# Zero-padded keys written by GpSimd, one crossbar DMA per head pair, and the gain product on ScalarE

## The chip, the cores and the metric

The kernel runs on one core of one Trainium2 chip. The metric is the device time of one execution in microseconds (us); lower is better. The median of three runs before the change is 489.74 us (489.65 to 492.26).

## What is computed

The reference is an attention with normalised queries and keys, followed by a two-layer network with a sigmoid gate. In short:

```python
def rmsnorm(x, g):
    rms = np.sqrt(np.mean(x * x, axis=-1, keepdims=True) + 1e-06)
    return x / rms * g
q_n, k_n = rmsnorm(q, g_q), rmsnorm(k, g_k)          # (8, 12, 448, 64)
scores = 1.0 / np.sqrt(64) * q_n @ k_n.transpose(0, 1, 3, 2)
attn = softmax(scores)
x = (attn @ v).transpose(0, 2, 1, 3).reshape(3584, 768)
h = x @ w_in                                          # 768 x 2048
out = (h * (1.0 / (1.0 + np.exp(-1.702 * h)))) @ w_out
```

Both gains act on the 64 channels of a head that the score product sums over. So g_q and g_k may be multiplied together and applied once, to the queries or to the keys.

## The kernel before, in words

**Tiling.** The attention works on 48 pairs of heads: 8 batches with 6 pairs each, and `i` numbers the pairs. A pair's 448 rows are 4 blocks of 112. Its two heads have 64 channels each, which fill 128 partitions once they are turned. The network follows batch by batch: for each of 8 batches 16 tiles of `w_in` (L485), and for two batches together 7 row tiles of `w_out` (L508).

**One pair, step by step.** `load` (L237, L242) brings q, k and v, from SyncE's queue (SP). `square` (L247) on ScalarE and `reduce` (L253) on VectorE give sums of squares. `seed` on VectorE and `rsqrt` on GpSimd make the inverse root, for three pairs together. `norm` (L291), on GpSimd, multiplies q (`gi` 0) and k (`gi` 1) and writes bf16 rows `qkn`, ordered by block, head and channel. Then the rows are turned, so that the channels lie on the partitions:

- pairs 0 to 11 (`ON_PE`): `turn_pe` (L309) on TensorE, `take_q` (L314) and `take_k` (L319) on VectorE;
- pairs 12 to 47: `turn_dma` (L326), a crossbar DMA in SyncE's queue that turns 8 blocks of 128 columns (4 of queries, 4 of keys) into `qT`, and then `pad` (L333) on VectorE, twice. Each `pad` copies the 64 partitions of one head's keys out of `qT` into `kz`, with the gains multiplied in. The other 64 partitions of each half of `kz` are zero from the start (L186, L187).

`score` (L343) multiplies `kz` with `qT` over all 128 partitions. The zero half keeps the other head out of the sum. `expo` (L348) on ScalarE takes the exponential, `values` (L355) multiplies with v, `divide` (L365, L366) on VectorE normalises, and a second crossbar DMA (L385) turns the result into `xT`, the input of the network. In the network, `tanh` (L494) runs on ScalarE, `gate` (L500) on VectorE, `take_out` (L518) on ScalarE.

**Rings.** `kz` and `qT` have 3 buffers each, `qkn` has 3, `raw` (the loaded q and k) has 7. A transposition of pair i therefore waits for the last score product of pair i-3, `norm` of pair i for the transposition of pair i-3, and the load of pair i for `norm` of pair i-7.

**What sets the order.** The order on each engine is written out ahead of the run by a planner, `_Order`. Each task has an engine, a planned duration, a key, and names that it depends on. The planner plays time forward, and a free engine takes the ready task with the smallest key. Each engine then runs its list in that order, so a late task holds back all that stands behind it in the same list. The planned durations matter for the order alone:

```python
for hp in range(2):
    od.add(("K", i, hp), "DVE", 540, lambda i=i, hp=hp: pad(i, hp), i - 2.5,
           deps=[("T", i)] + kz_free)
```

Here a `pad` is planned with 540 ns. The key of a score product is `i + kc / 4`, that of network work grows by 1 for every 5800 ns of planned matmuls. So TensorE's list interleaves network matmuls with attention. The network's work left over after the last pair makes up the end of the program.

Of the kernel before, what the change touches and what calls it, by code (L numbers as in the profile page):

```python
# [10 lines left out]
BF16 = mybir.dt.bfloat16  # L11
I32 = mybir.dt.int32
ALU = mybir.AluOpType
# [113 lines left out]
def kernel(  # L127
# [43 lines left out]
    for t, src in ((gq, g_q), (gk, g_k)):  # L171
        col = src.rearrange("(d o) -> d o", o=1)
        for lo in (0, 64):
# [1 line left out]
    gG = consts.tile([128, 1], FP32)  # L175


    N_ATT, N_KZ, N_V, N_RAW, N_SQ, N_QKN, N_QT = 3, 3, 4, 7, 2, 3, 3
    att_ring = [consts.tile([128, NS, 2, AW], BF16, name=f"att{j}", tag=f"att{j}")
                for j in range(N_ATT)]  # L180
    kz_ring = [consts.tile([128, 2, NS * SS], BF16, name=f"kz{j}", tag=f"kz{j}")
               for j in range(N_KZ)]
    vx_ring = [consts.tile([128, 2, NS, D + 1], BF16, name=f"vx{j}", tag=f"vx{j}")
               for j in range(N_V)]
    for t in kz_ring:
        nc.vector.memset(t[64:128, 0, :], 0.0)  # L186
        nc.vector.memset(t[0:64, 1, :], 0.0)  # L187
    for t in vx_ring:
        nc.gpsimd.memset(t[:, :, :, D:D + 1], 1.0)
    for t in att_ring:  # L190
# [8 lines left out]
    sq_p = pool("sq", N_SQ)  # L199
    stat_p = pool("stat", 3)  # L200
    small_p = pool("small", 2)
    qkn_p = pool("qkn", N_QKN)
    qT_p = pool("qT", N_QT)
    obs_p = pool("obs", 2)
    xt_p = pool("xt", 3)
    g_p = pool("g", 1)
# [16 lines left out]
            return link[0] - now + 500.0  # L223
        return lat

    raw, vraw, rs, qkn, qT, obs, xT = {}, {}, {}, {}, {}, {}, {}
    groups = [[0], [1], [2], [3, 4, 5]] + [list(range(j, j + 3)) for j in range(6, NG, 3)]
    group_of = {p: g for g in groups for p in g}
    ssq_of, sq_of = {}, {}
# [56 lines left out]

    def norm(i, gi):
        y, a = rs[i]
        if gi == 0:
            qkn[i] = qkn_p.tile([128, 2, NS, 2, D], BF16, tag="qkn", name="qkn")  # L290
        nc.gpsimd.tensor_tensor(  # L291
            out=qkn[i][:SS, gi],
            in0=raw[i][:SS, gi].rearrange("p h n d -> p n h d"),
            in1=y[:SS, a, gi].rearrange("p h n -> p n h").to_broadcast([SS, NS, 2, D]),
            op=ALU.mult)

    def vcast(i):
        vx = vx_ring[i % N_V][:SS].rearrange("p h n d -> p (h n) d")
# [6 lines left out]
    def turn_pe(i):  # L305
        tps[i] = ps_w.tile([128, 2, NS, SS], BF16, tag="w", name="t_ps")
        for gi in range(2):
            for s in range(NS):
                nc.tensor.transpose(tps[i][:, gi, s, :], qkn[i][:SS, gi, s, :, :],  # L309
                                    ident[:SS, :SS])  # L310

    def take_q(i):
        qT[i] = qT_p.tile([128, 2, NS * SS], BF16, tag="qT", name="qT")
        nc.vector.tensor_copy(out=qT[i][:, 0, :],  # L314
                              in_=tps[i][:, 0].rearrange("p n s -> p (n s)"))

    def take_k(i, hp):
        r = slice(64 * hp, 64 * hp + 64)
        nc.vector.tensor_scalar(out=kz_ring[i % N_KZ][r, hp, :],  # L319
                                in0=tps[i][:, 1].rearrange("p n s -> p (n s)")[r],  # L320
                                scalar1=gG[r, :], scalar2=None, op0=ALU.mult)

    def turn_dma(i):

        qT[i] = qT_p.tile([128, 2, NS * SS], BF16, tag="qT", name="qT")
        nc.sync.dma_start_transpose(  # L326
            out=qT[i][:, :, :].rearrange("p g (n s) -> p (g n) s", s=SS),
            in_=qkn[i][:SS].rearrange("s g n h d -> s (g n h d)"))

    def pad(i, hp):  # L330

        r = slice(64 * hp, 64 * hp + 64)
        nc.vector.tensor_scalar(  # L333
            out=kz_ring[i % N_KZ][r, hp, :].rearrange("p (n s) -> p s n", s=SS),
            in0=qT[i][r, 1, :].rearrange("p (n s) -> p s n", s=SS),
            scalar1=gG[r, :], scalar2=None, op0=ALU.mult)

    scs, os_ = {}, {}

    def score(i, kc):  # L340
        sc = scs[i, kc] = ps_sc.tile([128, 2, 512], FP32, tag="sc", name="sc")
        for hp in range(2):
            nc.tensor.matmul(sc[:SS, hp, :S],  # L343
                             lhsT=kz_ring[i % N_KZ][:, hp, kc * SS:(kc + 1) * SS],
                             rhs=qT[i][:, 0, :], start=True, stop=True)

    def expo(i, kc):
        nc.scalar.activation(out=att_ring[i % N_ATT][:SS, kc, :, :S],  # L348
# [47 lines left out]
    for i in range(NG):  # L396
        b = i // NP
        for w in range(3):
            od.add(("L", i, w), "ACTQ" if i == 0 and w == 1 else "SP", 400,
                   lambda i=i, w=w: load(i, w), i - 7 + 0.1 * w,  # L400
                   deps=[("V", i - N_RAW)] if w == 2 else [("N", i - N_RAW, 0), ("N", i - N_RAW, 1)],
                   lat=moved(830.0))
        parts = [slice(0, 1), slice(1, 2)] if i < 2 else [slice(0, 2)]
        for j, part in enumerate(parts):
            od.add(("S", i, j), "ACT", 920 / len(parts) + 80,
                   lambda i=i, p=part: square(i, p), i - 3,
                   deps=[("L", i, w) for w in range(part.start, part.stop)]
                   + [("R", i - N_SQ, 0), ("R", i - N_SQ, 1)])
            od.add(("R", i, j), "DVE", 1210 / len(parts) + 50,
                   lambda i=i, p=part: reduce(i, p), i - 2.8, deps=[("S", i, j)])  # L410
        if i == group_of[i][-1]:
            od.add(("Q0", i), "DVE", 400, lambda g=group_of[i]: seed(g), i - 2.7,
                   deps=[("R", p, j) for p in group_of[i] for j in range(2)])
            od.add(("Q", i), "POOL", 2300 if len(group_of[i]) > 1 else 1700,
                   lambda g=group_of[i]: rsqrt(g), i - 2.6, deps=[("Q0", i)])
        for gi in range(2):
            od.add(("N", i, gi), "POOL", 1080, lambda i=i, gi=gi: norm(i, gi), i - 2.4,
                   deps=[("Q", group_of[i][-1]), ("T", i - N_QKN)])
        od.add(("V", i), "POOL", 1000, lambda i=i: vcast(i), i - 1.6,
               deps=[("L", i, 2), ("P", i - N_V, 1, NS - 1)])  # L420
        kz_free = [("C", i - N_KZ, NS - 1)]
        if i < ON_PE:
            od.add(("T", i), "PE", 400, lambda i=i: turn_pe(i), i - 1.0,
                   deps=[("N", i, 0), ("N", i, 1)], lat=250, takes=("w", ("K", i, 1)))
            od.add(("KQ", i), "DVE", 400, lambda i=i: take_q(i), i - 2.0,
                   deps=[("T", i), ("C", i - N_QT, NS - 1)])
            for hp in range(2):
                od.add(("K", i, hp), "DVE", 460, lambda i=i, hp=hp: take_k(i, hp), i - 1.9,
                       deps=[("T", i), ("KQ", i), ("gG"), ("K", i, hp - 1)] + kz_free)
        else:  # L430
            od.add(("T", i), "SP", 400, lambda i=i: turn_dma(i), i - 10.0,
                   deps=[("N", i, 0), ("N", i, 1), ("C", i - N_QT, NS - 1)], lat=moved(1600.0))
            for hp in range(2):
                od.add(("K", i, hp), "DVE", 540, lambda i=i, hp=hp: pad(i, hp), i - 2.5,
                       deps=[("T", i)] + kz_free)
        for kc in range(NS):
            od.add(("C", i, kc), "PE", 380, lambda i=i, kc=kc: score(i, kc), i + kc / 4,
                   deps=[("K", i, 0), ("K", i, 1), ("KQ", i)], lat=250,
                   takes=("sc", ("E", i, kc)))
            od.add(("E", i, kc), "ACT", 917, lambda i=i, kc=kc: expo(i, kc), i + kc / 4 - 1,  # L440
                   deps=[("C", i, kc), ("P", i - N_ATT, 1, NS - 1)])
        for hp in range(2):
            for qs in range(NS):
                od.add(("P", i, hp, qs), "PE", 130, lambda i=i, hp=hp, qs=qs: values(i, hp, qs),
                       i + 0.8 + hp / 2 + qs / 8,
                       deps=[("E", i, kc) for kc in range(NS)] + [("V", i)]
                       + [("P", i, hp, qs - 1)], lat=250,
                       takes=("o", ("O", i, hp)) if qs == 0 else None)
            od.add(("O", i, hp), "DVE", 630, lambda i=i, hp=hp: divide(i, hp), i - 2,
                   deps=[("P", i, hp, NS - 1), ("B", i - 2)])  # L450
        xt_free = [("M", b - 3)] if i % NP == 0 else [("X", i - 1)]
        if i < ON_PE:
            od.add(("B", i), "PE", 200, lambda i=i: back_pe(i), i + 1.5,
                   deps=[("O", i, 0), ("O", i, 1)], lat=250, takes=("w", ("X", i)))
            od.add(("X", i), "DVE", 390, lambda i=i: take_x(i), i - 1, deps=[("B", i)] + xt_free)
        else:
            od.add(("X", i), "SP", 400, lambda i=i: back_dma(i), i - 10,
                   deps=[("O", i, 0), ("O", i, 1)] + xt_free, lat=moved(800.0))
            od.add(("B", i), "none", 0, lambda: None, i, deps=[("X", i)])
# [144 lines left out]
```

## Time and profile before

| | |
|---|---|
| median of 3 runs | 489.74 us |
| the profiled execution: its own time | 490.08 us |
| the profiled execution: span from first to last instruction | 488.3 us |
| mean granted TensorE clock | 0.982 of full speed |
| DMA | 63.36 MB in 95342 packets, mean 130 GB/s |

The rows of the profile come from the profiled execution. Engines: PE is TensorE's matmuls, PEld its weight loads, DVE is VectorE, ACT is ScalarE, POOL is GpSimd, SP is SyncE, whose queue (SPq) issues most DMAs. "o L355 <- DVE obs L366" means that the instruction of line 355, which writes `o`, started late because it had to wait for line 366 on DVE. A number in brackets at the end of a timeline row is the idle time of that engine just before the row, and what ended it.

### The profile page before, as it was taken

The numbers are of one execution on the slowest core, as the hardware profiler recorded it, in microseconds if no ns is written. First come the engines' busy times: TensorE is split into PE (matmuls) and PEld (weight loads), VectorE is DVE, ScalarE is ACT, GpSimd is POOL, SyncE is SP. The second block draws the span as 40 slices with busy tenths as digits, with TensorE's granted clock in tenths as the row PEclk, the third lists the DMA queues.
The fourth block names the chain that finished last, engine by engine and source line by source line (L and its number), as shares of the span: only waits on it lengthen the run. The fifth ranks groups of instructions, "written<-read, shape, count | busy, mean of one in ns | idle before, by whom it ended". The sixth has DMA issues, their size and how long they took to land.

```text
span 488.3 us, 9605 instructions
## 1 busy us (share of the span) xinstructions
PE 440.4 (90%) x3728; PEld 271.5 (56%) x3728; DVE 324.2 (66%) x536; ACT 305.1 (62%) x427; POOL 236.5 (48%) x327
## 2 busy tenths in 40 slices
PE   0667999987998898999989999989999999999995
PEld 0345666654565464566555565556666666565563
DVE  4478888995885568977888659966696636512500
ACT  3585998756785377775866667856676557723421
POOL 2899787596365364646546566656344310000000
PEclk9986999999999799999999999999999999999999
DMA  8999999646554458366464576454412432012022
GB/s 201 235 244 250 253 243 212 174 100 161 123 133 122 135 130 170 86 152 168 126 161 89 150 182 143 125 119 124 107 30 51 101 71 62 20 43 66 0 66 65
DMA packets 95342, 63.36 MB, mean 130 GB/s; under 512 B 54336, under 2 KB 91712, under 8 KB 95296
## 3 DMA queue, kind: packets, MB, share of 16 engines
q1 hardware_dynamic: 89488, 56.22, 47.0%
q0 software_dynamic: 5248, 6.29, 7.4%
q8 instruction: 29, 0.48, 0.4%
q10 hardware_dynamic: 560, 0.23, 0.3%
q14 instruction: 17, 0.14, 0.1%
HBM read 45.61 MB, written 11.01 MB: 116 GB/s over the span
## 4 chain that ended last, share of the span: by engine, by line
PE 45%; DVE 19%; POOL 14%; DMA 12%; issue 4%; ACT 3%; SPq 1%; ACTq 0%; POOLq 0%; DVEq 0%
PE op L508 19%; PE gp L485 15%; DVE kz L333 9%; POOL qkn L291 7%; PE sc L343 6%; DMA qT<-qkn 5%; PE o L355 5%; DVE ssq L253 4%; DMA raw<-in_k_dram 4%; DVE g L500 3%; DMA raw<-in_q_dram 2%; ACT sq L247 2%; POOL vx L300 2%; DVE obs L366 2%; POOL rs L283 1%
## 5 line engine op out<-in xcount | busy, mean ns | idle before, releaser
L348 ACT ACTIVATE att<-sc 112x896 bf16<-112x896 f32 x192 | 173.5, 915 | 61.3 <-PE sc L343 59.8
L508 PE MATMUL op<-w_out_s,g 128*128 128x384 bf16 x896 | 169.3, 328 | 0.1
L485 PE MATMUL gp<-xt,w_in_s 128*128 128x448 bf16 x768 | 162.9, 352 | 2.9 <-DVE g L500 2.9
L291 POOL TENSOR_TENSOR qkn<-raw,rs 112x512 bf16<-112x512 f32 x96 | 123.8, 1311 | 80.9 <-DMA qT<-qkn 80.2
L333 DVE TENSOR_SCALAR kz<-qT,gG 64x448 bf16<-64x448 bf16 x72 | 113.9, 1582 | 9.1 <-DMA qT<-qkn 8.3
L355 PEld LDWEIGHTS <-att 112*128 112x128 bf16 x1536 | 82.3, 99 | 57.2 <-issue 12.8
L343 PE MATMUL sc<-qT,kz 128*112 128x448 bf16 x384 | 108.2, 369 | 3.0 <-ACT att L348 2.1
L508 PEld LDWEIGHTS <-g 128*128 128x128 bf16 x896 | 81.8, 98 | 49.0 <-issue 1.7
L355 PE MATMUL o<-vx,att 112*128 112x65 bf16 x1536 | 92.8, 196 | 15.8 <-DVE obs L366 7.5
L485 PEld LDWEIGHTS <-w_in_s 128*128 128x128 bf16 x768 | 70.6, 97 | 60.8 <-issue 4.2
L500 DVE SCALAR_TENSOR_TENSOR g<-th,gp 128x448 bf16<-128x448 f32 x128 | 79.9, 633 | 34.9 <-ACT th L494 34.4
L494 ACT ACTIVATE th<-gp 128x448 f32<-128x448 f32 x128 | 69.5, 543 | 47.3 <-PE gp L485 46.3
L300 POOL TENSOR_TENSOR vx<-vraw,ones 112x512 bf16<-112x512 f32 x48 | 60.8, 1268 | 41.4 <-PE o L355 30.7
L253 DVE TENSOR_REDUCE ssq<-sq 112x16 f32<-112x1024 f32 (+1 forms) x50 | 58.4, 1172 | 21.3 <-ACT sq L247 17.9
L247 ACT ACTIVATE sq<-raw 112x1024 f32<-112x1024 f32 (+1 forms) x50 | 50.7, 1022 | 24.1 <-DMA raw<-in_k_dram 21.4
L365 DVE RECIPROCAL rcp<-o 112x4 f32<-112x4 f32 x96 | 17.6, 184 | 59.2 <-PE o L355 58.4
L518 ACT ACTIVATE osb<-op 128x384 f32<-128x384 f32 x56 | 27.3, 487 | 41.8 <-PE op L508 41.3
L343 PEld LDWEIGHTS <-kz 128*112 128x112 bf16 x384 | 43.7, 135 | 17.1 <-issue 3.9
L366 DVE TENSOR_TENSOR obs<-o,rcp 112x256 bf16<-112x256 f32 x96 | 40.7, 424 | 3.4
L309 PE MATMUL t_ps<-ident,qkn 112*128 112x112 bf16 x96 | 10.0, 247 | 18.8 <-POOL qkn L291 18.6
L309 PEld LDWEIGHTS <-qkn 112*128 112x128 bf16 x96 | 6.9, 113 | 22.6 <-POOL qkn L291 21.4
L276 POOL TENSOR_TENSOR rs<-magic,seed 112x48 int32<-112x48 int32 (+1 forms) x18 | 4.9, 271 | 29.7 <-DVE seed L268 29.5
(28 smaller groups left out, 91.7 us busy)
## 6 DMA issues: line engine op xcount, KB each, us to landing
raw<-in_q_dram SPq DMA_DIRECT2D x48, 224.0 KB, 3.2
vraw<-in_v_dram SPq DMA_DIRECT2D x48, 224.0 KB, 3.8
raw<-in_k_dram SPq DMA_DIRECT2D x47, 224.0 KB, 3.9
w_in_s<-in_moe_w_in_dram POOLq DMA_DIRECT2D x4, 768.0 KB, 12.6
w_out_s<-in_moe_w_out_dram POOLq DMA_DIRECT2D x4, 768.0 KB, 10.8
out_dram<-osb SPq DMA_DIRECT2D x8, 336.0 KB, 2.9
out_dram<-osb SPq DMA_DIRECT2D x8, 288.0 KB, 2.8
out_dram<-osb SPq DMA_DIRECT2D x8, 240.0 KB, 2.8
```

Of the source, the lines that this page charges most:

```text
L247: nc.scalar.activation(out=sq_of[i][:SS, part], in_=raw[i][:SS, part], func=ACT.Square)
L253: nc.vector.reduce_sum(out=ssq_of[g0][:SS, i - g0, part], in_=sq_of[i][:SS, part], axis=AX.X)
L291: nc.gpsimd.tensor_tensor(out=qkn[i][:SS, gi], in0=raw[i][:SS, gi].rearrange("p h n d -> p n h d"), in1=y[:SS, a, gi].rearrange("p h n -> ...
L300: nc.gpsimd.tensor_tensor(out=vx[:, :, :D], in0=vr, in1=ones[:SS, :].to_broadcast([SS, 2 * NS, D]), op=ALU.mult)
L333: nc.vector.tensor_scalar(out=kz_ring[i % N_KZ][r, hp, :].rearrange("p (n s) -> p s n", s=SS), in0=qT[i][r, 1, :].rearrange("p (n s) -> p ...
L343: nc.tensor.matmul(sc[:SS, hp, :S], lhsT=kz_ring[i % N_KZ][:, hp, kc * SS:(kc + 1) * SS], rhs=qT[i][:, 0, :], start=True, stop=True)
L348: nc.scalar.activation(out=att_ring[i % N_ATT][:SS, kc, :, :S], in_=scs.pop((i, kc))[:SS, :, :S], func=ACT.Exp)
L355: nc.tensor.matmul(os_[i, hp][:, qs, :], lhsT=att_ring[i % N_ATT][:SS, kc, hp, qs * SS:qs * SS + WIN], rhs=vx_ring[i % N_V][:SS, hp, kc, : ...
L485: nc.tensor.matmul(ps[:, :], lhsT=w_in_s[:, ki, m * 128:(m + 1) * 128], rhs=xT[b][:, ki, :], start=(ki == 0), stop=(ki == KI - 1))
L494: nc.scalar.activation(out=th[:, :], in_=gps[b, m][:, :], func=ACT.Tanh, scale=0.851)
L500: nc.vector.scalar_tensor_tensor(out=g_of[b // 2][:, m, lo:lo + S], in0=ths.pop((b, m))[:, :], scalar=1.0, in1=gps.pop((b, m))[:, :], op0= ...
L508: nc.tensor.matmul(ops[bp, tm, hf][:, :], lhsT=g_of[bp][:, ko, tm * 128:(tm + 1) * 128], rhs=w_out_s[:, ko, hf * HALF:(hf + 1) * HALF], st ...
```

## The change

GpSimd's `norm` writes into a row of 13 blocks of 128 columns, `row`: 4 blocks of queries, then 4 blocks with head 0's keys in their first 64 columns, then 4 with head 1's keys in their last 64. The columns between are zeroed once per buffer, by two GpSimd memsets ahead of the second `norm` of pairs 12, 13 and 14. `turn_dma` turns 12 blocks instead of 8, into one tile `qk` that replaces `qT` and `kz` and holds queries and both padded halves of the keys. `pad` is gone. The gains are multiplied into the queries in place by a new step, `scale_q`, an Identity activation on ScalarE with the gains as a scale for each partition. `score` reads both operands out of `qk`. For pairs 0 to 11 TensorE still turns the rows, and `take_q` and `take_k` write into `qk`. In the plan, the transposition's time of transfer goes from 1600 to 2400 ns, the two VectorE tasks of 540 ns go, and a ScalarE task of 540 ns with key `i - 1.5` comes.

```diff
+    qk_ring = [consts.tile([128, 3 * NS, SS], BF16, name=f"qk{j}", tag=f"qk{j}")
                for j in range(N_KZ)]
+    row_ring = [consts.tile([128, (3 * NS + 1) * 128], BF16, name=f"row{j}", tag=f"row{j}")
+                for j in range(N_QKN)]
+    def row_view(j, gi):
+        t = row_ring[j % N_QKN]
+        if gi == 0 or j < ON_PE:
+            t = t[:, gi * NS * 128:(gi + 1) * NS * 128]
+            return t.rearrange("p (n h d) -> p h n d", h=2, d=D)
+        both = t[:, NS * 128:].rearrange("p (h r) -> p h r", h=2)[:, :, :NS * 128]
+        return both.rearrange("p h (n c) -> p h n c", c=128)[:, :, :, :D]
...
+    for t in qk_ring:
+        nc.vector.memset(t[64:128, NS:2 * NS, :], 0.0)
+        nc.vector.memset(t[0:64, 2 * NS:, :], 0.0)
...
     def norm(i, gi):
         y, a = rs[i]
-        if gi == 0:
-            qkn[i] = qkn_p.tile([128, 2, NS, 2, D], BF16, tag="qkn", name="qkn")
+        if gi == 1 and ON_PE <= i < ON_PE + N_QKN:
+            c = row_ring[i % N_QKN][:, NS * 128:3 * NS * 128].rearrange("p (n c) -> p n c", c=128)
+            nc.gpsimd.memset(c[:, :NS, D:], 0.0)
+            nc.gpsimd.memset(c[:, NS:, :D], 0.0)
         nc.gpsimd.tensor_tensor(
-            out=qkn[i][:SS, gi],
-            in0=raw[i][:SS, gi].rearrange("p h n d -> p n h d"),
-            in1=y[:SS, a, gi].rearrange("p h n -> p n h").to_broadcast([SS, NS, 2, D]),
-            op=ALU.mult)
+            out=row_view(i, gi)[:SS], in0=raw[i][:SS, gi],
+            in1=y[:SS, a, gi].to_broadcast([SS, 2, NS, D]), op=ALU.mult)
...
     def turn_dma(i):
-        qT[i] = qT_p.tile([128, 2, NS * SS], BF16, tag="qT", name="qT")
-        nc.sync.dma_start_transpose(
-            out=qT[i][:, :, :].rearrange("p g (n s) -> p (g n) s", s=SS),
-            in_=qkn[i][:SS].rearrange("s g n h d -> s (g n h d)"))
-    def pad(i, hp):
-        r = slice(64 * hp, 64 * hp + 64)
-        nc.vector.tensor_scalar(
-            out=kz_ring[i % N_KZ][r, hp, :].rearrange("p (n s) -> p s n", s=SS),
-            in0=qT[i][r, 1, :].rearrange("p (n s) -> p s n", s=SS),
-            scalar1=gG[r, :], scalar2=None, op0=ALU.mult)
+        nc.sync.dma_start_transpose(out=qk_ring[i % N_KZ][:, :, :],
+                                    in_=row_ring[i % N_QKN][:SS, :3 * NS * 128])
+    def scale_q(i):
+        t = qk_ring[i % N_KZ][:, :NS, :]
+        nc.scalar.activation(out=t, in_=t, func=ACT.Identity, scale=gG[:, :])
...
             nc.tensor.matmul(sc[:SS, hp, :S],
-                             lhsT=kz_ring[i % N_KZ][:, hp, kc * SS:(kc + 1) * SS],
-                             rhs=qT[i][:, 0, :], start=True, stop=True)
+                             lhsT=qk_ring[i % N_KZ][:, NS * (1 + hp) + kc, :],
+                             rhs=qk_ring[i % N_KZ][:, :NS, :], start=True, stop=True)
...
             od.add(("T", i), "SP", 400, lambda i=i: turn_dma(i), i - 10.0,
-                   deps=[("N", i, 0), ("N", i, 1), ("C", i - N_QT, NS - 1)], lat=moved(1600.0))
-            for hp in range(2):
-                od.add(("K", i, hp), "DVE", 540, lambda i=i, hp=hp: pad(i, hp), i - 2.5,
-                       deps=[("T", i)] + kz_free)
+                   deps=[("N", i, 0), ("N", i, 1)] + kz_free, lat=moved(2400.0))
+            od.add(("KQ", i), "ACT", 540, lambda i=i: scale_q(i), i - 1.5,
+                   deps=[("T", i), ("gG")])
```

## Rows read from the trace of the kernel before

**Rows 1.** The page, part 1: busy time, share of the span, instructions of each engine.

```profile
PE 440.4 (90%) x3728; PEld 271.5 (56%) x3728; DVE 324.2 (66%) x536; ACT 305.1 (62%) x427; POOL 236.5 (48%) x327
```

**Rows 2.** Busy time of each engine in two long stretches, with the columns' header.

```profile
core 0: us, PE busy (x) PEld busy (x) DVE busy (x) ACT busy (x) POOL busy (x), PEclk, DMA share, GB/s
...
80.00:330.00 250.00, 232.69 (x1992) 143.11 (x1990) 194.48 (x289) 168.78 (x236) 147.11 (x177) 0.99 0.57 138
330.00:483.00 153.00, 153.00 (x1192) 92.89 (x1188) 73.03 (x121) 79.81 (x122) 28.89 (x30) 1.00 0.25 61
```

**Rows 3.** PE's waits from 80 us on: us in total, times, longest us.

```profile
PE o L355 <- DVE obs L366: 6.8, 4, 3.1
PE gp L485 <- DVE g L500: 2.9, 6, 0.9
PE o L355 <- POOL vx L300: 2.7, 3, 1.8
PE o L355 <- ACT att L348: 1.9, 2, 1.8
PE ot_ps L378 <- DVE obs L366: 1.3, 1, 1.3
PE o L355 <- POOL qkn L291: 1.3, 2, 0.8
```

**Rows 4.** Timeline around PE's longest wait: start us, us, engine line, what.

```profile
156.43 3.85 DVE L333 TENSOR_SCALAR kz<-qT,gG 64x448 bf16<-64x448 bf16 x2
...
160.31 0.18 DVE L365 RECIPROCAL rcp<-o 112x4 f32<-112x4 f32 x1
...
161.10 0.60 PE L355 MATMUL o<-vx,att 112*128 112x65 bf16 x8 [3.15 <-DVE obs L366]
```

**Rows 5.** Timeline around the wait that is put down to POOL vx.

```profile
323.62 1.39 DVE L333 TENSOR_SCALAR kz<-qT,gG 64x448 bf16<-64x448 bf16 x1
...
325.04 0.18 DVE L365 RECIPROCAL rcp<-o 112x4 f32<-112x4 f32 x1
...
325.83 0.41 PE L355 MATMUL o<-vx,att 112*128 112x65 bf16 x8 [1.84 <-POOL vx L300]
```

**Rows 6.** PE alone after the longest wait: busy us (count), granted clock, DMA.

```profile
160.00:165.00 5.00, 3.90 (x22) 0.50 0.38 72
165.00:170.00 5.00, 5.00 (x42) 0.82 0.64 200
```

**Rows 7.** Groups by line: busy us, mean ns of one, idle before and releasers.

```profile
L291 POOL TENSOR_TENSOR qkn<-raw,rs 112x512 bf16<-112x512 f32 x96 | 123.8, 1311 | 80.9 <-DMA qT<-qkn 80.2
L333 DVE TENSOR_SCALAR kz<-qT,gG 64x448 bf16<-64x448 bf16 x72 | 113.9, 1582 | 9.1 <-DMA qT<-qkn 8.3
...
L494 ACT ACTIVATE th<-gp 128x448 f32<-128x448 f32 x128 | 69.5, 543 | 47.3 <-PE gp L485 46.3 <-DVE g L500 0.6 <-DVE rcp L365 0.2
...
L247 ACT ACT_TABLE_LOAD x1 | 1.3, 1283 | 3.9 <-issue 3.9
...
L191 POOL MEMSET att<- 128x128 bf16 x3 | 0.5, 202 | 0.0
```

**Rows 8.** DMA issues: median us from issue to landing.

```profile
qT<-qkn SPq DMA_TRANSPOSE x36, 3.1
xt<-obs SPq DMA_TRANSPOSE x36, 2.5
```

**Rows 9.** Tile qkn: duration ns min/median/max, first and last start.

```profile
L291 POOL TENSOR_TENSOR qkn<-raw,rs x96: 1047/1058/2013, 13.2 to 380.6; 112x512 bf16<-112x512 f32 x96
...
L326 SPq DMA_TRANSPOSE qT<-qkn x36: 1221/1224/1914, 81.6 to 401.8; - x36
```

**Rows 10.** DVE's wait for the turned rows, 80 to 410 us: us, times, longest.

```profile
DVE kz L333 <- DMA qT<-qkn: 8.3, 8, 2.1
```

**Rows 11.** ACT's wait for loaded keys in the same stretch.

```profile
ACT sq L247 <- DMA raw<-in_k_dram: 16.8, 9, 4.6
```

More of the change, by code (lines that the diff above doesn't have):

```diff
@@ L175 @@
     gG = consts.tile([128, 1], FP32)
-    N_ATT, N_KZ, N_V, N_RAW, N_SQ, N_QKN, N_QT = 3, 3, 4, 7, 2, 3, 3
+    N_ATT, N_KZ, N_V, N_RAW, N_SQ, N_QKN = 3, 3, 4, 7, 2, 3
     att_ring = [consts.tile([128, NS, 2, AW], BF16, name=f"att{j}", tag=f"att{j}")
                 for j in range(N_ATT)]
-    kz_ring = [consts.tile([128, 2, NS * SS], BF16, name=f"kz{j}", tag=f"kz{j}")
+    qk_ring = [consts.tile([128, 3 * NS, SS], BF16, name=f"qk{j}", tag=f"qk{j}")
                for j in range(N_KZ)]
+    row_ring = [consts.tile([128, (3 * NS + 1) * 128], BF16, name=f"row{j}", tag=f"row{j}")
[7 more added lines that the diff above has]
+        return both.rearrange("p h (n c) -> p h n c", c=128)[:, :, :, :D]
     vx_ring = [consts.tile([128, 2, NS, D + 1], BF16, name=f"vx{j}", tag=f"vx{j}")
                for j in range(N_V)]
-    for t in kz_ring:
-        nc.vector.memset(t[64:128, 0, :], 0.0)
-        nc.vector.memset(t[0:64, 1, :], 0.0)
+    for t in qk_ring:
+        nc.vector.memset(t[64:128, NS:2 * NS, :], 0.0)
+        nc.vector.memset(t[0:64, 2 * NS:, :], 0.0)
     for t in vx_ring:
@@ L201 @@
     small_p = pool("small", 2)
-    qkn_p = pool("qkn", N_QKN)
-    qT_p = pool("qT", N_QT)
     obs_p = pool("obs", 2)
@@ L224, in moved @@
         return lat
-    raw, vraw, rs, qkn, qT, obs, xT = {}, {}, {}, {}, {}, {}, {}
+    raw, vraw, rs, obs, xT = {}, {}, {}, {}, {}
     groups = [[0], [1], [2], [3, 4, 5]] + [list(range(j, j + 3)) for j in range(6, NG, 3)]
@@ L308, in turn_pe @@
             for s in range(NS):
-                nc.tensor.transpose(tps[i][:, gi, s, :], qkn[i][:SS, gi, s, :, :],
-                                    ident[:SS, :SS])
+                nc.tensor.transpose(
+                    tps[i][:, gi, s, :],
+                    row_ring[i % N_QKN][:SS, (gi * NS + s) * 128:(gi * NS + s + 1) * 128],
+                    ident[:SS, :SS])
     def take_q(i):
-        qT[i] = qT_p.tile([128, 2, NS * SS], BF16, tag="qT", name="qT")
-        nc.vector.tensor_copy(out=qT[i][:, 0, :],
-                              in_=tps[i][:, 0].rearrange("p n s -> p (n s)"))
+        nc.vector.tensor_copy(out=qk_ring[i % N_KZ][:, :NS, :], in_=tps[i][:, 0])
     def take_k(i, hp):
         r = slice(64 * hp, 64 * hp + 64)
-        nc.vector.tensor_scalar(out=kz_ring[i % N_KZ][r, hp, :],
-                                in0=tps[i][:, 1].rearrange("p n s -> p (n s)")[r],
-                                scalar1=gG[r, :], scalar2=None, op0=ALU.mult)
+        nc.vector.tensor_scalar(out=qk_ring[i % N_KZ][r, NS * (1 + hp):NS * (2 + hp), :],
+                                in0=tps[i][r, 1], scalar1=gG[r, :], scalar2=None,
+                                op0=ALU.mult)
     def turn_dma(i):
-        qT[i] = qT_p.tile([128, 2, NS * SS], BF16, tag="qT", name="qT")
-        nc.sync.dma_start_transpose(
-            out=qT[i][:, :, :].rearrange("p g (n s) -> p (g n) s", s=SS),
-            in_=qkn[i][:SS].rearrange("s g n h d -> s (g n h d)"))
-    def pad(i, hp):
-        r = slice(64 * hp, 64 * hp + 64)
-        nc.vector.tensor_scalar(
-            out=kz_ring[i % N_KZ][r, hp, :].rearrange("p (n s) -> p s n", s=SS),
-            in0=qT[i][r, 1, :].rearrange("p (n s) -> p s n", s=SS),
-            scalar1=gG[r, :], scalar2=None, op0=ALU.mult)
+        nc.sync.dma_start_transpose(out=qk_ring[i % N_KZ][:, :, :],
[3 more added lines that the diff above has]
+        nc.scalar.activation(out=t, in_=t, func=ACT.Identity, scale=gG[:, :])
     scs, os_ = {}, {}
@@ L425 @@
             od.add(("KQ", i), "DVE", 400, lambda i=i: take_q(i), i - 2.0,
-                   deps=[("T", i), ("C", i - N_QT, NS - 1)])
+                   deps=[("T", i)] + kz_free)
             for hp in range(2):
```

## Prediction

> **What bounds the kernel now.** I read the busy shares first: TensorE works 90% of the span, the next engine, VectorE, 66% [rows 1]. Busy shares are averages, so I split the span where TensorE stops having gaps. From 330 to 483 us it is busy for all 153.0 us. From 80 to 330 us, where pairs are turned by the crossbar DMA, it is busy 232.7 of 250 us and VectorE 194.5, ScalarE 168.8, GpSimd 147.1 [rows 2]. So TensorE is the bound, its list is followed in order, and whatever gap is closed between 80 and 330 us moves the full last stretch forward by as much. No gap, no gain: the ceiling of any change that leaves the matmuls alone is what TensorE loses there.
>
> That loss is the list of TensorE's waits from 80 us on. They sum to 6.8 + 2.9 + 2.7 + 1.9 + 1.3 + 1.3 = 16.9 us [rows 3]. VectorE's results (`obs`, `g`) are named in 6.8 + 2.9 + 1.3 = 11.0 us of it. Next I looked at what VectorE does before such a wait. In the longest, two `pad` instructions take 3.85 us, and only then come the reciprocal and the division that free the PSUM tile `o`: TensorE stood 3.15 us [rows 4]. The 1.84 us put down to POOL `vx` has the same shape: a `pad` at 323.62, the reciprocal at 325.04 right behind it, the matmul at 325.83 [rows 5]. So I count it with VectorE: 11.0 + 1.8 = 12.8 us.
>
> One more loss isn't in that list. After the 3.15 us wait the granted clock is 0.50 for one 5 us window and 0.82 in the next [rows 6], so at the lower of its two levels (1.2 GHz) for part of the time. Priced from these rows: 3.90 us busy at half speed lose 1.95, 5.0 us at 0.82 lose 0.9, together 2.9 us. If the gap ahead of it goes, I expect this to go as well.
>
> **The change, part by part.**
>
> *The two pads leave VectorE.* 72 x 1.582 us = 113.9 us of its time [rows 7]. The plan had them at 540 ns each, so the order that was made is too tight for VectorE by a factor of nearly three, which is why `divide` and `gate` come late. Off the path this is worth nothing; on the path it is the 12.8 us above, plus the clock's 2.9: 15.7 us. What is late next on those waits is `reduce`, `gate` and `divide` themselves; they were planned near what they take, so I expect little of these gaps to come back. Bounds: zero (everything behind the pads is as late for another reason) and 16.9 + 2.9 = 19.8 us (all of TensorE's waits go).
>
> *`scale_q` comes on ScalarE.* 36 x 128 partitions x 448 elements, bf16 in place. No such row exists. Nearest is `tanh`, 128x448, 543 ns [rows 7], and I take that: 36 x 0.543 = 19.5 us on an engine that is busy 168.8 of 250 us [rows 2]. It is not on TensorE's path by itself; what counts is how much it delays the exponentials and `tanh` queued behind it. Upper bound for one: 0.543 plus two table loads of 1.283 us (out to another function table and back) = 3.1 us; the run before has a single table load in all [rows 7], and the nearest row has none, so I stay with it. Lower bound: a short instruction as hidden as `tanh` now, zero. The Trainium skill (ScalarE: Activation LUTs, section What ACT_TABLE_LOAD costs) prices a pointer scale at 93 ns above an immediate one, 652 ns here; by that the term would be 23.5 us instead of 19.5, and the end 0.4 us later at the rate found next.
>
> *The wait for the transposition moves with it.* Before, `pad` waited for it on VectorE 8 times, 8.3 us, at most 2.1 [rows 10]; now `scale_q` waits at the head of ScalarE's list, and behind it stand `expo`, `tanh`, `take_out` and `square`. How much of ScalarE's lateness reaches TensorE? ScalarE already waits 16.8 us, 9 times, for loaded keys [rows 11], and TensorE's waits on ScalarE are 1.9 us [rows 3]: 11%. So I charge (19.5 + 8.3) x 0.11 = 3.1 us. Ends: 0 and the whole 27.8.
>
> *The transposition grows from 8 blocks to 12.* It lands 3.1 us after issue, and the 4-block one (`xt`) after 2.5 [rows 8]: 0.15 us a block, so 3.7 us for 12, against 4.65 if it went purely by size and 3.1 if the fixed part were all. I take 3.7. The issue takes 1.22 us of SyncE's list [rows 9], for which I take the same value, at most 1.5 times it; loads, stores and the other transposition stand behind it there. The path of a pair gets no longer: landing and two pads were 3.1 + 2 x 1.58 = 6.3 us, landing and `scale_q` are 3.7 + 0.54 = 4.2. GpSimd waits for the landing too (80.2 us of idle ahead of `norm` [rows 7]); 0.6 us more makes the next `norm`, the loads behind the `raw` ring and so `square` later: 9 waits x 0.6 x 0.11 = 0.6 us. Cover: seven `raw` buffers and three of `row`; with them gone each of 36 pairs would show 0.6, 21.6 us.
>
> *GpSimd.* Same elements and the same runs of 64 in `norm`, written in another place. The shortest now is 1047 ns, the mean 1311, the longest 2013 [rows 7, 9]; I take the mean. At the longest, 72 x 0.7 = 50 us more would fit into its 80.2 us of waiting. Six memsets of 256 elements, nearest 202 ns for 128 [rows 7], between that and twice that: 1.2 to 2.4 us, in the same idle time. The memsets on VectorE stay as many and as large. Pairs 0 to 11 keep their instructions, and the score matmuls keep their shapes: zero, since tile sizes and rings of three are unchanged.
>
> **Sum.** -15.7 + 3.1 + 0.6 = -12.0 us against the profiled execution's own 490.08 (span 488.3 and 1.8 around it), so 478.1. The median of the runs lies 0.34 lower, so I forecast 477.7 us.
>
> **Rivals.**
>
> 1. *All gaps close.* The pads delay everything, GpSimd and loads too, and ScalarE hides its part: 490.08 - 19.8 - 0.34 = 469.9. For it: in rows 5 a wait named for GpSimd was VectorE's. Against: the 1.9 us on ScalarE has another cause, late keys. Chance 0.15.
>
> 2. *No change: ScalarE loses what VectorE won.* If every `scale_q` delays the exponentials behind it by its full 0.543 us, 19.5 us come back, against 19.8 at most: 489.4. For it: the exponentials feed TensorE in order, with two score buffers. Against: ScalarE idles 81 of 250 us there [rows 2]. The Trainium skill (ScalarE: Activation LUTs, section Rules for kernel authors) speaks for this side: it wants a multiplication on VectorE, up to about three times as fast there in bf16. This case's rows differ: 1582 ns for half the partitions on VectorE, 543 for all on ScalarE [rows 7]. Chance 0.14.
>
> 3. *Slower: the wait for the landing at the head of ScalarE's list.* Place: `scale_q` of each of 36 pairs. Price: if it waits as long as `pad` at worst, 2.1 us, plus 0.6 for the longer landing, plus 0.54 of work = 3.2, less what ScalarE can absorb; its nine waits for keys averaged 1.9 us and hardly reached TensorE. So 1.3 x 36 = 48 us: 477.7 - 3.7 + 48 = 522. It decides once the wait is above about 1.4 us in most pairs. Against: only 8 of 72 pads waited at all, and pairs are turned well ahead: 36 issues from 81.6 to 401.8 [rows 9] are 9.1 us a pair, and three buffers allow the landing almost two pairs of time. Chance 0.11.
>
> **Numbers.** The forecast has 0.60. Faster by over 0.5% (about what a measurement of this kernel can tell from no change; below 487.3) are the forecast and rival 1: 0.75. Rival 2 is within 0.5%: 0.14. Rival 3 is slower: 0.11. The range starts just below rival 1, at 469, and goes up to 489: there about 11 of the 27.8 us that ScalarE could cost at most, or half of the landing's 21.6, are lost. It holds the forecast, rival 1 and the lower part of rival 2; outside lie rival 3 and the rest of rival 2.
>
> **What would show it.** Right: no `pad` rows and about 210 us busy on VectorE; TensorE's waits on `obs` and `g` from 80 us on below 3 us, no granted clock of 0.5 after 80 us, `scale_q` at 0.54 to 0.65 us and a landing at 3.7 us. ScalarE's wait for the turned rows should stay under 9 us in all. Wrong: more than one table load; ScalarE waiting for the transposition over 20 us; TensorE's waits on `att` growing by more than 5 us; or waits on `obs` unchanged without pads, so that they weren't the cause.

## The result, and the profile after

The changed kernel takes 466.68 us (median of 4 runs, 466.25 to 469.82), against 490.9 us for the kernel before on the same chip: ratio 0.952, 95% interval 0.9467 to 0.9573. The profiled execution took 466.25 us with a span of 464.5, 23.8 us less span than before. The forecast was 477.7, with a range of 469 to 489. So the direction was right, and the gain came out twice as large, beyond the range's fast end.

Part 1 of the page of the kernel after, which answers to [rows 1]:

```profile
PE 434.7 (94%) x3728; PEld 271.7 (59%) x3728; DVE 217.5 (47%) x464; ACT 322.7 (69%) x463; POOL 197.7 (43%) x333
```

VectorE has lost 106.7 us of work, ScalarE has 17.6 more. GpSimd has 38.8 us less, which the forecast had left at nothing. Busy time of each engine in the two stretches, in the columns of [rows 2]:

```profile
80.00:330.00 250.00, 249.52 (x2188) 157.37 (x2187) 122.50 (x254) 198.12 (x286) 122.55 (x198) 1.00 0.69 162
330.00:459.00 129.00, 129.00 (x982) 77.92 (x980) 38.09 (x83) 67.52 (x106) 14.38 (x14) 1.00 0.26 57
```

TensorE has practically no gap left between 80 and 330 us: 249.5 of 250 us, at full granted clock. PE's waits from 80 us on are one row now, where [rows 3] had six:

```profile
PE sc L349 <- ACT att L354: 0.4, 1, 0.4
```

The groups of the new or moved steps (busy us, mean ns of one, idle before):

```profile
L305 POOL TENSOR_TENSOR row<-raw,rs 112x512 bf16<-112x512 f32 x96 | 98.1, 1042 | 95.3 <-DMA qk<-row 86.9 <-issue 7.9
...
L312 POOL TENSOR_TENSOR vx<-vraw,ones 112x512 bf16<-112x512 f32 x48 | 49.9, 1042 | 40.5 <-PE o L361 30.4 <-issue 7.4 <-DMA vraw<-in_v_dram 2.6
...
L342 ACT ACTIVATE qk<-qk,gG 128x448 bf16<-128x448 bf16 x36 | 24.0, 667 | 3.8 <-DMA qk<-row 3.7
...
L304 POOL MEMSET row<- 128x256 bf16 x3 | 0.9, 312 | 0.0
```

The DMA issues of the two transpositions (median us to landing), and tile `qk`'s row of the issue on SyncE:

```profile
qk<-row SPq DMA_TRANSPOSE x36, 4.0
xt<-obs SPq DMA_TRANSPOSE x36, 2.6
```

```profile
L337 SPq DMA_TRANSPOSE qk<-row x36: 1281/1386/2359, 81.5 to 378.0; - x36
```

ScalarE's waits for DMAs between 80 and 410 us, where [rows 10, 11] had 8.3 us (on VectorE) and 16.8:

```profile
ACT sq L259 <- DMA raw<-in_k_dram: 5.2, 7, 1.3
ACT qk L342 <- DMA qk<-row: 3.7, 5, 1.6
```

**Where the 23.8 us came from.** From 80 us to the end of its last matmul TensorE needed 483.0 - 80 = 403.0 us before and needs 459.2 - 80 = 379.2 us now, 23.8 us less. In one window from 80 us on these are 3179 matmuls before and 3169 after; the sums of the two stretches above count those that lie across 330 us twice. The 10 fewer are worth some 1.2 us (379 / 3169 each), so 22.6 us were won after 80 us. Waits that the profile names give 16.9 - 0.4 = 16.5 of it, the clock 2.9 (the granted clock is 1.00 now from 80 us to the last matmul). The remaining 3.2 us are almost all counted as busy time in the profile before, though TensorE did no more in it. The other 1.2 us lie ahead of 80 us, where the change does next to nothing; by then the runs of this study have begun between 545 and 563 matmuls, so I read no cause into them.

Another view bears on those hidden 3.2 us: the waits of the weight loads (PEld), from 80 us on, before and after ("issue" stands where the engine waited for nothing that the profile shows).

```profile
PEld L355 <- issue: 12.4, 14, 3.5
PEld L485 <- issue: 4.2, 6, 1.1
PEld L355 <- DVE obs L366: 2.2, 2, 1.9
PEld L355 <- ACT att L348: 2.2, 2, 1.9
PEld L508 <- issue: 1.7, 10, 0.2
PEld L378 <- DVE obs L366: 1.7, 1, 1.7
PEld L355 <- PE sc L343: 1.5, 2, 1.0
PEld L355 <- PE op L508: 0.9, 1, 0.9
PEld L508 <- DVE g L500: 0.5, 1, 0.5
```

```profile
PEld L349 <- issue: 0.6, 1, 0.6
PEld L361 <- DVE obs L372: 0.5, 2, 0.3
PEld L490 <- issue: 0.4, 1, 0.4
PEld L513 <- issue: 0.2, 1, 0.2
```

They sum to 27.3 us before, in 39 stops, and 1.7 after, while the matmuls' own list had 18 stops and 16.9 us. The stop that the matmuls' list has at 3.15 us [rows 4] has 3.5 here. I read the two lists as bounds: the ends of the matmuls in this profile are modelled, so a stop can look shorter there than it was, and a short one can vanish; a load, on the other side, may stand while matmuls still stream. The 22.6 us that were won, less 2.9 for the clock, are 19.7, and lie between what the two lists lost, 16.5 and 25.6. Worked in the same way, against the changed kernel, the six later runs whose profiled executions take 7 us or more longer (E2, E3, E5, E10, E11, E12) lie between their two lists as well: E12, for one, loses 18.1 us, and its lists are 16.4 and 21.8 longer.

### The profile page after: what moved, and what is told of

Read it like the earlier page. It is cut to its first block, busy times and chain, and to the rows that moved or that the text cites. A ratio compares the mean times of both kernels' runs of the same rounds, so it can differ in the third digit from the quotient of the medians.

```text
span 464.5 us, 9577 instructions
## 1 busy us (share of the span) xinstructions
PE 434.7 (94%) x3728; PEld 271.7 (59%) x3728; DVE 217.5 (47%) x464; ACT 322.7 (69%) x463; POOL 197.7 (43%) x333
## 4 chain that ended last, share of the span: by engine, by line
PE 83%; POOL 8%; DMA 4%; issue 2%; DVE 2%; ACT 1%; SPq 0%; ACTq 0%; POOLq 0%; DVEq 0%
PE op L513 31%; PE gp L490 29%; PE sc L349 13%; PE o L361 9%; POOL row L305 4%; DMA vraw<-in_v_dram 1%; DMA raw<-in_q_dram 1%; DVE ssq L265 1%; DMA raw<-in_k_dram 1%; DMA gq<-in_g_q_dram 1%; POOL seed L292 1%; POOL rs L295 1%; POOL seed L291 1%; POOL seed L293 1%; ACT sq L259 0%
## 5 line engine op out<-in xcount | busy, mean ns | idle before, releaser
L305 POOL TENSOR_TENSOR row<-raw,rs 112x512 bf16<-112x512 f32 x96 | 98.1, 1042 | 95.3 <-DMA qk<-row 86.9
L349 PE MATMUL sc<-qk 128*112 128x448 bf16 x384 | 108.0, 369 | 3.4 <-ACT att L354 2.5
L505 DVE SCALAR_TENSOR_TENSOR g<-th,gp 128x448 bf16<-128x448 f32 x128 | 78.2, 616 | 63.8 <-ACT th L499 63.4
L361 PE MATMUL o<-vx,att 112*128 112x65 bf16 x1536 | 90.9, 195 | 2.6 <-ACT att L354 1.9
L312 POOL TENSOR_TENSOR vx<-vraw,ones 112x512 bf16<-112x512 f32 x48 | 49.9, 1042 | 40.5 <-PE o L361 30.4
L349 PEld LDWEIGHTS <-qk 128*112 128x112 bf16 x384 | 44.4, 135 | 18.2 <-issue 4.9
L523 ACT ACTIVATE osb<-op 128x384 f32<-128x384 f32 x56 | 27.3, 487 | 38.8 <-PE op L513 38.6
L342 ACT ACTIVATE qk<-qk,gG 128x448 bf16<-128x448 bf16 x36 | 24.0, 667 | 3.8 <-DMA qk<-row 3.7
L321 PE MATMUL t_ps<-ident,row 112*128 112x112 bf16 x96 | 10.0, 248 | 17.7 <-POOL row L305 17.5
L321 PEld LDWEIGHTS <-row 112*128 112x128 bf16 x96 | 6.8, 113 | 21.5 <-POOL row L305 20.3
```

What stands on the lines that cost most here:

```text
L305: nc.gpsimd.tensor_tensor(out=row_view(i, gi)[:SS], in0=raw[i][:SS, gi], in1=y[:SS, a, gi].to_broadcast([SS, 2, NS, D]), op=ALU.mult)
L312: nc.gpsimd.tensor_tensor(out=vx[:, :, :D], in0=vr, in1=ones[:SS, :].to_broadcast([SS, 2 * NS, D]), op=ALU.mult)
L349: nc.tensor.matmul(sc[:SS, hp, :S], lhsT=qk_ring[i % N_KZ][:, NS * (1 + hp) + kc, :], rhs=qk_ring[i % N_KZ][:, :NS, :], start=True, stop=True)
L361: nc.tensor.matmul(os_[i, hp][:, qs, :], lhsT=att_ring[i % N_ATT][:SS, kc, hp, qs * SS:qs * SS + WIN], rhs=vx_ring[i % N_V][:SS, hp, kc, : ...
L505: nc.vector.scalar_tensor_tensor(out=g_of[b // 2][:, m, lo:lo + S], in0=ths.pop((b, m))[:, :], scalar=1.0, in1=gps.pop((b, m))[:, :], op0= ...
```

## Experiments

Theory A is the forecast's: VectorE's slow pads at the head of its list make TensorE wait. Rivals: B, the order that the plan gives; C, GpSimd slowed down by the pads; D, the shorter path of a pair. All ratios below are to the kernel before on the same chip.

**E1 and E9: the pads in order of address.** Nothing else of the change.

```diff
-            out=kz_ring[i % N_KZ][r, hp, :].rearrange("p (n s) -> p s n", s=SS),
-            in0=qT[i][r, 1, :].rearrange("p (n s) -> p s n", s=SS),
+            out=kz_ring[i % N_KZ][r, hp, :],
+            in0=qT[i][r, 1, :],
```

> The kernel before, where each pad reads and writes its 448 columns in order of address instead of stepping from block to block; 8 blocks turned, two pads behind them, plan and order unchanged. Theory A (what cost the time is VectorE's 114 us in the slow pads, at the head of its list): a pad falls below 0.5 us, VectorE is busy some 80 us less, TensorE's waits on obs and g from 80 us on fall below 3 us, time 466 to 473. Rival D (the gain comes from the shorter path of a pair, one transposition and one short step in place of a transposition and two pads): most of the loss stays, 482 to 491. Rival C (pads slow GpSimd down, so norm and the loads are late): norm's mean tells; if it stays at 1.3 us while the time falls, C is out.

468.72 us, ratio 0.9568 (0.9532 to 0.9604). The groups of `norm` and of the pads, then PE's waits from 80 us on, and tile `kz`'s durations of a pad (min/median/max), before and in E1:

```profile
L291 POOL TENSOR_TENSOR qkn<-raw,rs 112x512 bf16<-112x512 f32 x96 | 100.2, 1067 | 82.5 <-DMA qT<-qkn 81.6 <-POOL qkn L291 0.2
...
L333 DVE TENSOR_SCALAR kz<-qT,gG 64x448 bf16<-64x448 bf16 x72 | 46.2, 642 | 7.1 <-DMA qT<-qkn 6.3
```

```profile
PE o L355 <- ACT att L348: 2.0, 2, 1.4
PE o L355 <- DVE obs L366: 0.4, 1, 0.4
```

```profile
L333 DVE TENSOR_SCALAR kz<-qT,gG x72: 1224/1406/2151, 90.0 to 407.0; 64x448 bf16<-64x448 bf16 x72
```

```profile
L333 DVE TENSOR_SCALAR kz<-qT,gG x72: 318/466/1229, 90.5 to 385.4; 64x448 bf16<-64x448 bf16 x72
```

Two lines give nine tenths of the gain. The pads still wait for the turned rows, the 8-block transposition and two pads still make up a pair's path, and every engine's order is that of before, task by task. So D is out, and with it the need for padding in the transposition. What cost the time was the pads' step from block to block. With it went three things at once, and E1 doesn't tell them apart: a pad's length (the median falls from 1406 ns to 466, the mean from 1582 to 642), GpSimd's lost time (`norm` falls from 1311 ns to 1067, so this run doesn't rule out C), and the gap between the plan's 540 ns and what a pad takes (B). VectorE is busy 63 us less, not the 80 expected. To compare it with the change itself, both ran again on one chip:

> The kernel after unchanged, on one chip with the dense pads, to tell the two apart: 466 to 467.5.

> The kernel before with pads in order of address, again. Theory A leaves 72 pads of about 0.64 us on VectorE (46 us in place of none) and TensorE 2.4 us of waits from 80 us on: 1 to 3 us slower than the kernel after, 467.5 to 470. If moving the padding into the transposition buys nothing beyond the pads' speed, the two intervals meet.

467.54 us, ratio 0.9514 (0.9477 to 0.9552), for the change, and 468.55, 0.953 (0.9496 to 0.9563), for the dense pads. The medians stand in the expected order (the first is 0.04 us above its range), but the intervals meet: an advantage of the larger change over the two lines isn't shown.

**E2: the old work put back on VectorE.** `ballast` is a copy of `pad` from the turned keys into a scratch tile; its own lines are left out here.

```diff
...
+            for hp in range(2):
+                od.add(("K", i, hp), "DVE", 540, lambda i=i, hp=hp: ballast(i, hp), i - 2.5,
+                       deps=[("T", i), ("gG")])
```

> The kernel after, with two instructions like the old pads put back on VectorE for each of pairs 12 to 47 (same shape, same step from block to block, same key and planned 540 ns, behind the transposition), whose result goes to a scratch tile that nothing reads. Theory A: they take 1.2 to 2.1 us each again, TensorE's waits on VectorE come back (8 to 12 us), time 482 to 492. Rival D: no reader waits for them and the new path is as short as after: 466 to 470. Rival C: norm goes back to about 1.3 us; time as under A, so C isn't told from A by this run alone.

482.63 us, ratio 0.9847 (0.9812 to 0.9882): 16 of the 24 us come back ((0.9847 - 0.952) x 490), though nobody reads the result. PE's waits from 80 us on, then the groups:

```profile
PE o L370 <- POOL vx L312: 2.9, 2, 2.0
PE gp L502 <- DVE g L517: 2.9, 4, 1.9
PE o L370 <- POOL rs L295: 2.4, 2, 1.6
PE o L370 <- DVE obs L381: 1.7, 2, 0.9
PE ot_ps L393 <- DVE obs L381: 0.7, 1, 0.7
PE o L370 <- POOL row L305: 0.7, 1, 0.7
```

```profile
L305 POOL TENSOR_TENSOR row<-raw,rs 112x512 bf16<-112x512 f32 x96 | 120.3, 1274 | 73.2 <-DMA qk<-row 70.0 <-issue 2.6
L348 DVE TENSOR_SCALAR scratch<-qk,gG 64x448 bf16<-64x448 bf16 x72 | 108.0, 1500 | 13.8 <-DMA qk<-row 13.0
```

TensorE waits 11.3 us again, 5.3 of them named for VectorE. Three things come with the ballast: 108 us on VectorE, 13.0 us of waiting for turned rows at the head of its list, and a `norm` of 1274 ns. A fourth is the plan: the ballast has the name of the pads' task, so the planner puts the scores behind it, and at 540 ns. E5, E10 and E11 take the first three apart; each has two instructions a pair in the same place, and the order on every engine is the same in the four.

**E5: VectorE's time alone.** The ballast is `reduce_sum` over a constant.

> The kernel after with two instructions put on VectorE for each of pairs 12 to 47 that take its time but touch neither the turned rows nor the gains: sums over 112x1280 fp32 elements of a constant, some 1.5 us each if reduce's 1.216 us for 1024 elements scales, in the place that the pads had in the order (key i - 2.5, planned 540 ns). They need no transposition and nobody reads them. Theory A (VectorE's time at the head of its list): TensorE's waits on VectorE come back, 478 to 486, as with the pad-like ballast (482.6). Rival C (GpSimd slowed down by the pads): if norm stays at 1.04 us the time stays at 466 to 470, and the 16 us of the pad-like ballast were GpSimd's.

**E10: time and the collision with GpSimd.** The pad-like ballast reads a constant tile.

> The kernel after with the pad-like ballast (same shape, step, place and planned time), but reading a constant tile: it no longer waits for the turned rows, and still runs beside GpSimd. The pad-like ballast cost 16 us, the sums of the same length on constants 6. If the rest is the wait for turned rows at the head of VectorE's list: 471 to 475, as for the sums. If it is the collision with GpSimd (norm at 1.27 instead of 1.04 us, and the ballast itself stretched): 479 to 484, with norm near 1.27 again.

**E11: time and the wait.** `reduce_sum` over turned keys.

> The kernel after with two sums a pair as ballast, 112x1344 elements, some 1.5 us, read out of the turned keys: they wait for the transposition at the head of VectorE's list, and should leave GpSimd alone (norm 1.04 us). If the wait for turned rows is what made the pad-like ballast cost 10 us more than sums on constants: 479 to 484. If it was the collision with GpSimd: 471 to 476.

The groups of the ballast and of `norm` in E5, E10 and E11:

```profile
L349 DVE TENSOR_REDUCE busy_out<-busy_in 112x20 f32<-112x1280 f32 x72 | 106.6, 1480 | 0.9
L305 POOL TENSOR_TENSOR row<-raw,rs 112x512 bf16<-112x512 f32 x96 | 98.2, 1043 | 96.9 <-DMA qk<-row 93.2 <-issue 3.1
```

```profile
L305 POOL TENSOR_TENSOR row<-raw,rs 112x512 bf16<-112x512 f32 x96 | 116.3, 1232 | 78.8 <-DMA qk<-row 75.4 <-issue 2.7
L350 DVE TENSOR_SCALAR scratch<-fixed,gG 64x448 bf16<-64x448 bf16 x72 | 102.0, 1417 | 0.7
```

```profile
L348 DVE TENSOR_REDUCE busy_out<-qk 112x12 f32<-112x1344 bf16 x72 | 111.5, 1549 | 19.0 <-DMA qk<-row 18.0
L305 POOL TENSOR_TENSOR row<-raw,rs 112x512 bf16<-112x512 f32 x96 | 98.1, 1042 | 100.3 <-DMA qk<-row 96.1 <-issue 3.5
```

A pad-like ballast in E10 (min/median/max):

```profile
L350 DVE TENSOR_SCALAR scratch<-fixed,gG x72: 1222/1252/2095, 91.3 to 393.3; 64x448 bf16<-64x448 bf16 x72
```

| ballast on the kernel after | time, us | ratio (interval) | (ratio - 0.952) x 490, us |
|---|---|---|---|
| E5: time | 473.0 | 0.9645 (0.961 to 0.968) | 6 |
| E10: time, collision | 475.4 | 0.9705 (0.9647 to 0.9762) | 9 |
| E11: time, wait | 476.6 | 0.9725 (0.9658 to 0.9792) | 10 |
| E2: time, collision, wait | 482.6 | 0.9847 (0.9812 to 0.9882) | 16 |

My expectations for E5, E10 and E11 missed, since each theory wanted one cause. The same 105 us or so on VectorE cost about 6 us alone, which is clear of the noise; the order that comes with every ballast, made for 540 ns, is inside these 6. Collision and wait add about 3 and 4, but the intervals of E10 and E11 overlap each other's and E5's, so neither is shown by itself. E2 lies above all three: with both there it costs 6 to 7 us more than with either (1.3 of it is the lower granted clock, 0.81 and 0.85 between 145 and 155 us, which those three don't have).

**E6: GpSimd slower, VectorE free.** A short multiplication behind each `norm` of pairs 12 to 47 and each `vcast`.

> The kernel after with GpSimd made slower by about as much as beside the pads: a short multiplication of 112x48 elements (0.28 us) behind each norm of pairs 12 to 47 and behind each vcast, 120 x 0.28 = 34 us, without a change of the plan. Theory A: GpSimd waits 86.9 us for transpositions anyway, and TensorE hardly notices: 465.5 to 469. Rival C: 473 to 482.

467.9 us, ratio 0.9548 (0.9515 to 0.9581), with 31.8 us added (120 x 265 ns). The interval reaches into that of the kernel after. C alone is out. Whether a slow GpSimd matters beside a busy VectorE is E10's question, and there the noise hides the answer.

**E3: the plan alone.** Kernel before, a pad planned with 1400 ns.

```diff
-                od.add(("K", i, hp), "DVE", 540, lambda i=i, hp=hp: pad(i, hp), i - 2.5,
+                od.add(("K", i, hp), "DVE", 1400, lambda i=i, hp=hp: pad(i, hp), i - 2.5,
```

> The kernel before with one number changed: a pad is planned with 1400 ns (its median in the trace) instead of 540, so only the order on the engines changes. Theory A: VectorE still has its 114 us and they still stand ahead of others; part of the loss can be moved but not removed: 482 to 491. Rival B (it is the order that the plan gave, made with a wrong duration, that makes TensorE wait): 466 to 476.

482.27 us, ratio 0.9859 (0.9812 to 0.9905). One number is worth 7 us: part of what the pads cost was an order made for pads of 540 ns. B carries a part, not the whole; and E1 keeps the order of before, which costs nothing that shows once the pads take about what it was made for.

**E12: the scores wait for VectorE again.** Kernel after without `scale_q`, with the gains multiplied into the turned keys, in place, by two instructions stepped like the old pads.

> The kernel after, with the gains multiplied into the turned keys on VectorE by two instructions shaped and stepped like the old pads, in place, instead of scale_q on ScalarE. So the transposition is the new one of 12 blocks, and VectorE has the old work, and the scores wait for it again (in the pad-like ballast nobody did: 482.6). If the last 8 us of the gain are the scores' wait for the pads: 488 to 493. If they are the order that the plan makes, which also differs from that of before: 480 to 485.

486.94 us (10 runs), ratio 0.9919 (0.9891 to 0.9948): between the two expectations. It lies some 3.5 us above E2, where no score waits for VectorE. Two more things differ from E2, so this isn't the wait's price alone: `scale_q` is gone from ScalarE, and TensorE's order differs in 35 of its 952 places. About 4 us to the kernel before are left, and whether they are the order or the transposition's layout stays open.

**E7: `scale_q` twice**, the second into a scratch tile.

> The kernel after with the gain activation on ScalarE done a second time, into a scratch tile that nobody reads: 36 x 0.667 = 24 us more on ScalarE, outside the plan. If ScalarE's added time costs what the prediction charged (11% of it), 2.6 us: 468 to 471. If it is hidden, as the 0.4 us of TensorE's waits on ScalarE in the kernel after say: 466 to 467.5. Rival 2 of the prediction (all of it delays the exponentials): 485 to 491.

468.54 us, ratio 0.9561 (0.9529 to 0.9593); PE's waits from 80 us on:

```profile
PE o L364 <- ACT att L357: 1.9, 5, 0.7
PE o L364 <- DVE obs L375: 0.9, 1, 0.9
```

Another 24 us on ScalarE cost about 2 (8%), and the interval overlaps that of the kernel after: this doesn't tell 11% from nothing. Rival 2 of the prediction is out.

**E4: the gains on VectorE**, one instruction in order of address, planned there with 300 ns.

```diff
-        nc.scalar.activation(out=t, in_=t, func=ACT.Identity, scale=gG[:, :])
+        nc.vector.tensor_scalar(out=t, in0=t, scalar1=gG[:, :], scalar2=None, op0=ALU.mult)
...
-            od.add(("KQ", i), "ACT", 540, lambda i=i: scale_q(i), i - 1.5,
+            od.add(("KQ", i), "DVE", 300, lambda i=i: scale_q(i), i - 2.5,
```

> The kernel after with the gain product on VectorE (one instruction on 128x448 in place, in order of address, planned 300 ns, key i - 2.5) instead of ScalarE. Theory A: where this short step stands hardly matters, since TensorE waits only 0.4 us on ScalarE from 80 us on: 465 to 468, the step below 0.5 us on VectorE. If ScalarE's 24 us had a price that the waits do not show (rival: ScalarE is the next bound), it comes out 2 us or more below the kernel after, under 464.5. If the step is as slow as a pad was (1.5 us), 36 of them cost 54 us of VectorE: 468 to 474.

466.15 us, ratio 0.9515 (0.9478 to 0.9551), not told apart from the change. Tile `qk`, min/median/max:

```profile
L342 DVE TENSOR_SCALAR qk<-qk,gG x36: 326/364/1222, 90.3 to 382.0; 128x448 bf16<-128x448 bf16 x36
```

So ScalarE was no better place than VectorE. In E12 the gain product stands on VectorE too, in two stepped instructions of 1545 ns on average, and takes 486.94 us: what mattered was that the work go in order of address and be short.

Put together, the pads' step from block to block is the cause (E1, E9), and no one theory carries its price: of some 24 us, VectorE's time with the order that comes with it brings back 6 (E5), with collision and wait for turned rows 16 (E2), and with scores that need the result 20 (E12).

## Why the prediction was wrong, point by point

- **TensorE is the bound, and gaps closed move the end one for one.** Right: its gaps went, and the end with them.
- **"That loss is the list of TensorE's waits" and the ceiling of 19.8 us.** This is the step that failed: it took the list for the whole of what TensorE loses, and so put the range's fast end too high. 22.6 us were won, where the ceiling was 19.8: 16.5 of the list's 16.9, 2.9 of the clock, and 3.2 us of stops that sit almost wholly inside time counted as busy.
- **12.8 of the 16.9 us go with the pads.** Undersized: 16.5 went. The waits that were named for GpSimd and left standing went with the stepped pads: E1's profile has none, E2's has 6.0 us again. The 1.9 us named for ScalarE fell to 0.4 (2.0 in E1). ScalarE's wait for loaded keys fell from 16.8 us to 5.2, but E2 loses 16 us with 6.4 of it, so by which path TensorE's waits hung on the pads stays open.
- **The clock, 2.9 us.** Right: no granted clock below 1.00 between 80 us and the last matmul.
- **`scale_q`, 543 ns, and 3.1 us charged.** It takes 667 ns; the estimate of 652 from the figures of the Trainium skill (ScalarE: Activation LUTs, What ACT_TABLE_LOAD costs) was nearer than the row that I took. The charge was not due: TensorE waits 0.4 us on ScalarE (1.7 in E8's profile of the same kernel), and E4, with the product off ScalarE, isn't told apart. The 11% came from waits of up to 4.6 us; `scale_q` waits five times, 1.6 us at most.
- **The longer transposition, 0.6 us charged.** It lands after 4.0 us instead of the 3.7 taken, and its issue takes 1.39 us; nothing of it is seen on TensorE.
- **GpSimd unchanged.** Wrong: `norm` fell from 1311 to 1042 ns, because the pads had stretched it, and the prediction had no term for that. A slower `norm` alone costs next to nothing (E6); beside a busy VectorE it may be 3 us (E10 less E5, not clear of the noise). The memsets (312 ns) lay within their bounds.
- **Rivals.** The first came true, 3 us beyond its number; it had 0.15. The second and third didn't: TensorE waits 0.4 us on ScalarE, and no `scale_q` waited long.

Summed up, for the profiled execution: forecast -12.0, measured -23.8. The difference of 11.8 is 3.7 of named gaps that I left standing, 3.7 of charges that weren't due, 3.2 that the list of waits doesn't have and 1.2 ahead of 80 us. The mechanism, VectorE's pads making TensorE wait, was right in the main; the sizes of these terms were not.

## What to carry to other kernels

Before moving an instruction to another engine, ask why it is slow: here the step that two `rearrange` calls made took a pad to three times the length, and taking them out gave nine tenths of what the larger change gave. Where TensorE is the bound, read a ceiling from the waits of its weight loads and from the matmuls done in a stretch as well as from the matmuls' waits, which are the lower end. Where an order is planned ahead, hold each planned duration against the trace's; one wrong number was 7 us.

## What I had not expected of the hardware

- A `tensor_scalar` on 64 x 448 bf16 that steps 224 bytes from element to element took 1224 ns at least in the kernel before; in order of address, in E1, 318. The Trainium skill (VectorE: DVE Perf Modes, Rules for kernel authors) names bf16 in dense steps of one as the way to most throughput; these two figures agree.
- The strided pads and GpSimd stretch each other: `norm` takes 1042 ns where VectorE has no pads, beside them 1216 (E3) to 1311; a strided pad took 1222 ns at least (E10) and up to 2151. Beside dense pads `norm` keeps 1067 ns, and the pads stretch up to 1229. The Trainium skill (SBUF — State Buffer, Who interferes with whom) says of a VectorE instruction in a two-port mode and a GpSimd one that whichever is issued first gets the port pair that they share, and that the other blocks until it is done. No run here shows the mode. By that rule a pad takes at most one `norm` on top of its own time, 1042 + 318 = 1360 ns for a dense one and 1042 + 1222 = 2264 for a strided one (estimates from these rows); the longest, 1229 and 2151, lie below. Sums on VectorE left `norm` at 1043 ns; the same section of the Trainium skill says that `tensor_reduce` never contends with GpSimd on trn2.
